# Block 1's lag product moved from the scan stage's lead-in into attention's last unit, and block 1's basis loaded after attention's last transposes

## Chip, cores and metric

The kernel runs on one core of one Trainium2 chip. The metric is device time in microseconds of one execution, taken as the median over several runs of the same built program. The core has five engines with their own instruction streams: PE (matmul), ACT (activations and copies), DVE (vector), POOL (general) and SP, which here only issues DMAs. Engines wait for each other by semaphores. A DMA is issued by the stream of one engine, in the order of that stream; a DMA whose wait isn't met holds up everything behind it on that engine. In this kernel SP and POOL issue nearly all DMAs; what SP issues runs as queue q1, what POOL issues as queue q0.

## What is computed

The reference is forward and backward of a gated sum of two branches over one sequence of 2048 tokens with 576 channels. Its core:

```python
x = A_x
g = _sigmoid((x * gate_w).sum(-1, keepdims=True))
a = _A_ref(x, A_wqkv, A_wo)      # attention, 32 heads of 18
b = _B_ref(x, B_A_re, ..., B_Dskip)   # S4: convolution with a kernel K(d, l)
return g * a + (1 - g) * b
```

`_B_ref` makes for each channel d the kernel `K = einsum("dn,dnl,dn->dl", C, exp(dt*A*l), dt*B).real` with 128 complex states and convolves it with the sequence. The outputs are the value and the gradients of twelve inputs (x, the attention weights, the S4 parameters, the gate), all in bf16.

## The kernel before

The kernel has four stages: projections (to about 150 us of the profiled span), attention forward and backward (to about 2097 us), the S4 branch forward and backward as a chunked scan (to about 2530 us), and a final stage that makes weight gradients and outputs.

**Attention** works in 32 units (8 groups of 4 heads, 4 query blocks of 512 each) of 32 steps. One loop over the step number `G` writes out the instructions of all engines by hand. A unit's backward part runs 39 steps (`OFF`) behind its forward part, so the last unit's backward part fills the steps `NTOT+7` to `NTOT+38`, where `NTOT` is the first step after all forward work. In every step of the backward part PE makes score products (`ps_P`), ACT exponentiates them (`eb`, L1387), and DVE multiplies (`ds`, L1392) the score gradients. The gradient tile of key block `i` (0 to 15, finished every second step) is turned by a DMA transpose on SP (`dsT<-ds`, L1400), 16 of 128x128 for some blocks and 12 for others, where PE turns the rest (`turn_p`, L1095). Its turned form is read by the key-gradient matmuls (`accK`). Finished gradients are turned the same way (`gT`, L1069) and packed and stored by POOL.

**Jobs hung on steps.** Work of the next stage is hung on steps of attention's last unit by `at(("pre", NTOT + x), f)`: f is written out just ahead of step `NTOT + x`, on each engine behind what the earlier steps put there. Memory for it becomes free as pools of attention's tiles are closed (`pt_close`).

**The scan stage** works in 18 blocks of 32 channels. For each block `b` there are:
- `m_load(b)` (L614, L615): the input block `xs` in two DMAs of 512 KB and the gradient block `gyp` of 128 KB. `xs` has one buffer, `gyp` two (by `b % 2`).
- `m_part(b)`: the lag product of the two, 32 matmuls into one bank (`psM`), copied by ACT into `mst` (L628) and written to DRAM as `Md_d` (L629, 288 KB).
- `m_skw(b)` (L641): `Md_d` read back skewed, in four DMAs of 64 KB, into `skw`, which has one buffer.
- `m_sum(b)`: eight small matmuls of `skw`; `m_fin(b)` (L652 to L654): ACT puts their result into the columns of `RX`. `uv(b, h)` (PE, ACT L708) multiplies the turned basis with `RX`, so it follows `m_fin(b)`.
- `load_en(b, h)` (L689): the basis `E1n` of half a block (h = 0, 1), 1 MB; in the lead-in it is issued in four pieces of 256 KB. `turn_e(b, h)` (L671, L672) turns it on PE and copies it out on DVE or ACT. `k0(b)` reads it as well.
- `scan` (DVE L733 to L738): the recurrences, started by `scan_open` (L714). Then `rw1`, `rw2` (DVE L753 `wab`, L758 `Rw`), `pairs1`, `pairs2` (DVE `pq`).
- `t0_load(b)` (L863): the kernel matrix `T0w`, 1 MB, read from `Kp_d`, which `k0_out` has just written.

A **lead-in** ahead of the block loop (L1455 to L1482) brings blocks 0 and 1 up to the scan: `k0(0)`, then the turns, lag sums and `uv` of blocks 0 and 1. There SP's order is written by hand too: the DMAs stand as the lines stand. In the block loop (from L1483) turn `i` scans the second half of block `i` and the first half of block `i + 1`, makes `m_sum(i + 2)`, `m_part(i + 3)`, and loads from POOL.

Before, only block 0's lag product is in attention's last unit: `m_load(0)` at x = 15, `m_part(0)` at 21, `m_skw(0)` at 25. The sixteen pieces of basis of blocks 0 and 1 go out one a step at x = 23 to 38, between the transposes, and `m_load(1)` at x = 40. `m_part(1)` and `m_skw(1)` stand in the lead-in between `turn_e(0, 1)` and `uv(0, 1)`; `m_part(2)` and `m_skw(2)` between `uv(1, 0)` and `uv(1, 1)`.

Of the kernel before, what the change touches and what calls it, by code (L numbers as in the profile page):

```python
# [20 lines left out]
def build(tc, aps, dbg_aps=None, stages=("s1", "attn", "post", "s4", "final")):  # L21
    nc = tc.nc
# [6 lines left out]
    def mm(out, lhsT, rhs, start=True, stop=True, **kw):  # L29
        return nc.tensor.matmul(out, lhsT=lhsT, rhs=rhs, start=start, stop=stop, **kw)  # L30
# [31 lines left out]
    with ExitStack() as gctx:  # L62
# [525 lines left out]
        def load_rx(xb, dma=nc.gpsimd.dma_start):  # L588
            d0 = xb * XB
            RXn = Q["pl"].tile([P, 2 * NB, XB], BF, tag="RXn", bufs=1, name="RXn")  # L590
            dma(RXn[:, 0:NB, :], xr_d[:, :, d0:d0 + XB])
            dma(RXn[:, NB:2 * NB, :], gyr_d[:, :, d0:d0 + XB])
            RXs[xb] = [RXn, None]
# [14 lines left out]
        def m_load(b, dma=nc.gpsimd.dma_start):  # L608
            xs = xss[b] = Q["pl"].tile([P, NSUB, SUB, CB], BF, tag="xs", bufs=1, name="xs")
            n = NSUB // 2  # L610
            for y in range(2):
                src = bass.AP(tensor=xb_d.tensor, offset=xb_d[b:b + 1, y * n:y * n + 1, 0:1].offset,
                              ap=[[XR * SUB * CB, NB], [SUB * CB, NSUB], [1, n * SUB * CB]])
                dma(xs[:, y * n:(y + 1) * n].rearrange("p e t c -> p (e t c)"), src)  # L614
            dma(Q["gyp2"][b % 2][:, SUB:2 * SUB, :].rearrange("p t c -> p (t c)"), gyb_d[b])  # L615

        def m_part(b):
            gyp = Q["gyp2"][b % 2]
            xs = xss[b]
            psM = Q["psM"]()  # L620
            for q in range(4):
                for g_ in range(4):
                    for u in range(2):
                        dd = 8 * q + 2 * g_ + u
                        mm(psM[32 * g_:32 * (g_ + 1), q, :].rearrange("p (e t) -> p e t", t=SUB), lhsT=gyp[:, (1 - u) * SUB:(3 - u) * SUB, dd],
                           rhs=xs[:, ::-1, ::-1, dd], start=(u == 0), stop=(u == 1), tile_position=(0, 32 * g_))
            mst = Q["mst"]
            nc.scalar.copy(mst[:, :, 0:P], psM)  # L628
            Q["mdma"](Md_d[b], mst)  # L629

        def dkp(b):
            return Q["misc2"][b % 2][:, 12 * CB:13 * CB]
# [3 lines left out]
        def m_skw(b):  # L636
            skw = skws[b] = Q["pl"].tile([P, 4, P], F32, tag="skw", name="skw")
            for q in range(4):
                src = bass.AP(tensor=Md_d.tensor, offset=Md_d[b:b + 1, 0:1, q:q + 1, SUB - 1:SUB].offset,
                              ap=[[SUB * 4 * MW, NSUB], [4 * MW - 1, SUB], [1, P]])  # L640
                Q["mdma"](skw[:, q, :], src)  # L641

        def m_sum(b):
            skw = skws.pop(b)
            for v in range(CB // 8):
                mm(dkp(b)[:, v * 8:v * 8 + 8], lhsT=skw[:, v, :], rhs=Q["sel"])

        def m_fin(b):
            RX = RXs[b // 2][1]
            o = (b % 2) * CB  # L650
            pk = dkp(b)
            nc.scalar.copy(RX[:, o:o + CB, CDK], pk)  # L652
            nc.scalar.mul(RX[:, o:o + CB, CDK + 1], pk, Q["l0col"])
            nc.scalar.copy(Q["dDs_row"][:, b * CB:(b + 1) * CB], pk[0:1, :])  # L654

        def blk(b):
            if b not in BK:
                B_ = BK[b] = dict(E={}, En={})
            return BK[b]
# [16 lines left out]
        def load_par(b, dma=nc.gpsimd.dma_start):  # L676
            par = pars_[b] = Q["pl"].tile([P, 10, XB], F32, tag="par", bufs=2, name="par")
            dma(par, par_d[:, 0:10, b * XB:(b + 1) * XB])
# [4 lines left out]
        def load_en(b, h, dma=nc.gpsimd.dma_start, pieces=1):  # L683
            dG = b * CB + h * GS
            En = blk(b)["En"][h] = Q["en", (2 * b + h) % 6 // 2].tile([P, GS, 2, P], BF, tag="E1n", bufs=2, name="E1n")
            n = GS // pieces

            def piece(x):
                dma(En[:, x * n:(x + 1) * n].rearrange("p (g c) r n -> p g (c r n)", c=EQ),  # L689
                    E_d[:, (dG + x * n) // EQ:(dG + (x + 1) * n) // EQ, 0:EQ * 2 * P])  # L690
            piece(0)
            return piece

        def uv(b, h):
            B_ = blk(b)
            if h == 0:
                B_["UV"] = Q["pw"].tile([P, 2, NCOL, CB], BF, tag="UV", bufs=3, name="UV")
            UV = B_["UV"]
            E_ = B_["E"].pop(h)
            RX = RXs[b // 2][1]  # L700
            off = (b % 2) * CB + h * GS
            for q in range(2):
                for ri in range(2):
                    pr = Q["ps"].tile([P, NCOL, 8], F32, tag="bk", bufs=4, name="uvp")
                    for c_ in range(8):
                        mm(pr[:, :, c_], lhsT=E_[:, q * 8 + c_, ri, :], rhs=RX[:, off + q * 8 + c_, :])
                    c0 = h * GS + q * 8
                    nc.scalar.mul(UV[:, ri, :, c0:c0 + 8], pr, -1.0 if ri == 0 else 1.0)  # L708
# [172 lines left out]
        def open_en(x):  # L881
            cm = tc.tile_pool(name=f"s4en{x}", reuse_waits="tile", bufs=1, side="right")
            Q["en", x] = cm.__enter__()
            rights.append(cm)
# [65 lines left out]
        if "attn" in stages:  # L950
# [5 lines left out]
            with ExitStack() as ctx:  # L956
# [157 lines left out]
                NST = 2 * NT  # L1114
                NU = NG * NQ
                OFF = NST + 7
# [4 lines left out]
                def at(n, f):  # L1121
                    todo.setdefault(n, []).append(f)
# [116 lines left out]
                NTOT = NU * NST  # L1239
# [23 lines left out]
                def pt_close(nm, then):  # L1263
                    pts[nm][0].__exit__(None, None, None)
                    then()

                Q["psM"] = lambda: apsp.tile([P, 4, P], F32, tag="accO", name="psM")
                enp = {}

                def en_first(b, h):  # L1270
                    enp[b, h] = load_en(b, h, nc.sync.dma_start, pieces=4)

                for x, f in ((15, lambda: pt_close("a", open_loads)), (15, lambda: m_load(0, nc.sync.dma_start)), (17, lambda: load_rx(0, nc.sync.dma_start)),
                             (21, lambda: m_part(0)), (23, lambda: pt_close("b", lambda: open_en(0))),
                             (25, lambda: m_skw(0)), (31, lambda: pt_close("c", lambda: open_en(1))),
                             (29, lambda: load_par(0, nc.sync.dma_start)), (33, lambda: load_par(1, nc.sync.dma_start)),
                             (OFF + NST // 16 - 1, lambda: m_load(1, nc.sync.dma_start))):
                    at(("pre", NTOT + x), f)
                for q, (b, h) in enumerate(((0, 0), (0, 1), (1, 0), (1, 1))):
                    at(("pre", NTOT + 23 + 4 * q), lambda b=b, h=h: en_first(b, h))  # L1280
                    for y in range(1, 4):
                        at(("pre", NTOT + 23 + 4 * q + y), lambda b=b, h=h, y=y: enp[b, h](y))
                for G in range(NTOT + OFF + 24):
                    now[0] = G
                    for f in todo.pop(("pre", G), []):
# [2 lines left out]
                    if G < NTOT:  # L1288
                        u, s = divmod(G, NST)
                        g, b = units[u]  # L1290
# [11 lines left out]
                    if r1:  # L1302
                        g, b, i, j0 = r1
# [14 lines left out]
                    elif 0 <= m_ < NTOT // 8:  # L1318
                        u_, kq = divmod(m_, NQ)
                        g, b = units[u_]  # L1320
                        if slot in SLOTS:
                            nm, burst, h = SLOTS[slot]
# [17 lines left out]
                    if r2:  # L1340
                        g, b, s2 = r2
# [16 lines left out]
                    if G % 8 in (0, 3, 4, 7) and G >= 3:  # L1358
                        i_ = (G - 3) // 8 * 4 + {3: 0, 4: 1, 7: 2, 0: 3}[G % 8]
                        u_, i_ = divmod(i_, NT)  # L1360
                        if 0 <= u_ < NU:
                            g, b = units[u_]
# [50 lines left out]
        if "s4" in stages:  # L1413
# [8 lines left out]
            with ExitStack() as ctx:  # L1422
# [27 lines left out]
                with tc.manual_schedule(engines={mybir.EngineType.SP}):  # L1450
# [6 lines left out]
                    turn_e(0, 0, 0, 4, dve_copy)  # L1457
                    m_sum(0)
                    m_fin(0)
                    uv(0, 0)  # L1460
                    prep_rx(1, dve_copy)
                    load_rx(1, nc.sync.dma_start)
                    turn_e(0, 1, 0, 4, dve_copy)
                    m_part(1)
                    m_skw(1)
                    m_load(2, nc.sync.dma_start)
                    uv(0, 1)
                    turn_e(1, 0, 0, 4, dve_copy)
                    scan_open(0)
# [1 line left out]
                    turn_e(1, 1, 0, 4)  # L1471
                    m_sum(1)
                    m_fin(1)
                    load_en(2, 1, nc.sync.dma_start)
                    uv(1, 0)
                    m_part(2)
                    m_skw(2)
                    uv(1, 1)
                    scan_open(1)
                    m_load(3, nc.sync.dma_start)  # L1480
                    prep_rx(2)
                    wk_cast(1)  # L1482
                    for i in range(NBLK):  # L1483
# [37 lines left out]
                        if i + 2 >= NBLK:  # L1521
                            y = 2 * (i + 2 - NBLK)
# [348 lines left out]
```

## Time and profile before

| | us |
|---|---|
| median of 3 runs | 2687.24 (2683.43 to 2697.16) |
| the profiled execution | 2685.73 |
| its span, first to last instruction | 2683.9 |

Busy time by stretch, in us, with the granted clock of PE (1.00 is full speed), the busy share of the DMA engines and what they moved:

| stretch | us | PE | DVE | ACT | clock | DMA share | GB/s |
|---|---|---|---|---|---|---|---|
| 150 to 2000, attention | 1850 | 1665.99 | 1647.65 | 1837.72 | 0.99 | 0.85 | 162 |
| 2050 to 2097, its tail | 47 | 28.18 | 26.89 | 18.77 | 0.67 | 1.14 | 237 |
| 2097 to 2146, lead-in | 49 | 32.31 | 27.91 | 24.20 | 0.71 | 0.70 | 177 |
| 2146 to 2530, block loop | 384 | 367.88 | 369.20 | 328.74 | 0.98 | 0.86 | 254 |
| 2530 to 2684, final stage | 154 | 143.76 | 97.96 | 27.07 | 0.98 | 0.87 | 204 |

A share over 1 comes about because packets in flight on one DMA engine overlap. In the rows of the profile, `L1392 DVE ... ds<-ps_P,PT` reads: line 1392 of the kernel, engine, output and inputs, partitions times elements. A bracket `[3.34 <-DMA skw<-Md_d]` behind a row of a timeline is the engine's idle time ahead of it and what ended it. Rows named SPq are SP's issues, with the time from the start of an issue to the next: that includes waiting.

SP's issues around the end of attention, whole lines of its timeline (start, us, what):

```profile
2052.67 1.42 SPq L1400 DMA_TRANSPOSE dsT<-ds  x1
2054.13 1.07 SPq L689 DMA_DIRECT2D E1n<-E_d  x2
2055.30 2.22 SPq L1400 DMA_TRANSPOSE dsT<-ds  x1
2057.61 2.58 SPq L641 DMA_DIRECT2D skw<-Md_d  x4
2065.86 3.99 SPq L1400 DMA_TRANSPOSE dsT<-ds  x1
2090.95 1.82 SPq L1400 DMA_TRANSPOSE dsT<-ds  x1
2092.83 1.96 SPq L614 DMA_DIRECT2D xs<-xb_d  x2
2099.55 0.53 SPq L689 DMA_DIRECT2D E1n<-E_d  x1
2106.87 0.32 SPq L863 DMA_DIRECT2D T0w<-Kp_d  x1
2120.71 2.54 SPq L641 DMA_DIRECT2D skw<-Md_d  x4
```

The transposes, the basis pieces and the loads of the scan stage share this one queue. The row of 2092.83 is `m_load(1)`, the one of 2120.71 is `m_skw(1)`.

### The profile page before, as it was taken

The numbers are of one execution on the slowest core, as the hardware profiler recorded it, in microseconds if no ns is written. First come the engines' busy times: TensorE is split into PE (matmuls) and PEld (weight loads), VectorE is DVE, ScalarE is ACT, GpSimd is POOL, SyncE is SP. The second block draws the span as 40 slices with busy tenths as digits, with TensorE's granted clock in tenths as the row PEclk, the third lists the DMA queues.
The fourth block names the chain that finished last, engine by engine and source line by source line (L and its number), as shares of the span: only waits on it lengthen the run. The fifth ranks groups of instructions, "written<-read, shape, count | busy, mean of one in ns | idle before, by whom it ended". The sixth has DMA issues, their size and how long they took to land.

```text
span 2683.9 us, 69949 instructions
## 1 busy us (share of the span) xinstructions
PE 2404.7 (90%) x27411; PEld 1137.9 (42%) x27411; DVE 2293.8 (85%) x4090; ACT 2350.8 (88%) x2744; POOL 1818.0 (68%) x2829
## 2 busy tenths in 40 slices
PE   8799998998899899889888989989887699999999
PEld 4433333333333333333333333333232499998756
DVE  5648999999989999989999989989897589999964
ACT  5489999999999999999999999999995399999221
POOL 0278888888888888888888888887831045555431
PEclk9879999999999999999999999999996699999999
DMA  7637789879979978997898899789679889998895
GB/s 232 196 99 156 154 159 181 167 153 181 172 152 170 183 160 159 178 172 153 165 178 154 161 172 170 153 163 177 143 140 183 191 244 256 259 262 253 261 261 128
DMA packets 1157013, 486.63 MB, mean 181 GB/s; under 512 B 1071061, under 2 KB 1110598, under 8 KB 1154378
## 3 DMA queue, kind: packets, MB, share of 16 engines
q1 hardware_dynamic: 1110650, 341.49, 64.4%
q0 software_dynamic: 44016, 135.16, 18.3%
q10 hardware_dynamic: 2016, 5.51, 0.6%
q8 instruction: 214, 3.51, 0.6%
q14 instruction: 117, 0.96, 0.1%
HBM read 146.27 MB, written 93.80 MB: 89 GB/s over the span
## 4 chain that ended last, share of the span: by engine, by line
ACT 40%; PE 28%; DVE 18%; issue 6%; DMA 4%; POOL 2%; SPq 1%; ACTq 0%; DVEq 0%; POOLq 0%
ACT eb L1387 23%; ACT PT L1382 14%; DVE ds L1392 7%; PE ps_P L30 7%; PE accV L30 2%; PE ps_dx L30 2%; PE turn_p L1095 2%; PE ps_dwq L30 2%; DVE tz L733 2%; PE ps_proj L30 2%; DVE wab L753 2%; PE yp L30 2%; PE accK L30 1%; DVE dvacc L1149 1%; DVE tz L736 1%
## 5 line engine op out<-in xcount | busy, mean ns | idle before, releaser
L1392 DVE TENSOR_TENSOR ds<-ps_P,PT 128x512 bf16<-128x512 f32 x2048 | 1312.3, 683 | 125.5 <-PE ps_P L30 86.8
L1387 ACT ACTIVATE eb<-ps_P 128x1024 bf16<-128x1024 f32 x1024 | 1099.9, 1074 | 34.8 <-PE ps_P L30 34.5
L1382 ACT ACTIVATE PT<-ps_P 128x1024 bf16<-128x1024 f32 x1024 | 1105.0, 1080 | 21.7 <-PE ps_P L30 20.3
L30 PE MATMUL ps_P<-dOaT,VaT_g 32*128 32x512 bf16 x2048 | 581.9, 388 | 31.5 <-DVE ds L1392 16.1
L506 POOL TENSOR_TENSOR et<-eG,eT 128x448 f32<-128x448 f32 x576 | 542.2, 961 | 10.7
L30 PE MATMUL ps_P<-QaT_g,KaT_g 32*128 32x512 bf16 x2048 | 402.9, 386 | 136.5 <-ACT PT L1382 121.8
L30 PE MATMUL ps_P<-KaT_g,QaT_g 32*128 32x512 bf16 x2048 | 406.0, 389 | 1.6 <-ACT eb L1387 0.6
L30 PEld LDWEIGHTS <-KaT_g 32*128 32x128 bf16 x2048 | 147.6, 91 | 467.5 <-issue 451.4
L506 POOL TENSOR_TENSOR Eo<-et,et 128x448 bf16<-128x448 f32 x288 | 327.0, 1135 | 20.8
L30 PEld LDWEIGHTS <-QaT_g 32*128 32x128 bf16 x2048 | 116.1, 91 | 285.3 <-issue 262.4
L30 PE MATMUL accV<-eb,dOa 128*32 128x512 bf16 x2048 | 185.0, 394 | 27.2 <-ACT eb L1387 27.1
L30 PE MATMUL accO<-PT,Vtok_g 128*32 128x512 bf16 x2048 | 207.4, 394 | 0.0
L30 PE MATMUL accK<-dsT,Qtok_g 128*32 128x256 bf16 x4096 | 162.3, 279 | 14.5 <-DMA dsT<-ds 12.4
L30 PE MATMUL accQ<-ds,Ktok_g 128*32 128x512 bf16 x2048 | 161.6, 394 | 2.3 <-DVE dvacc L1149 2.2
L30 PEld LDWEIGHTS <-Vtok_g 128*32 128x32 bf16 x2048 | 52.7, 93 | 222.7 <-issue 222.7
L1100 DVE COPY dsT<-turn_p 128x1024 bf16<-128x1024 bf16 (+1 forms) x216 | 139.2, 644 | 2.1 <-PE turn_p L1095 2.1
L1095 PE MATMUL turn_p<-ident_bf,ds 128*128 128x128 bf16 x1664 | 134.1, 223 | 1.5 <-DVE gb L1167 0.8
L672 ACT COPY E1e<-etp 128x1024 bf16<-128x1024 bf16 x132 | 125.2, 1059 | 2.6 <-PE etp L671 2.6
L506 POOL TENSOR_TENSOR et<-eT 128x32 f32<-128x32 f32 (+3 forms) x288 | 115.9, 422 | 11.4
L1047 POOL TENSOR_TENSOR dOa<-dO_b,rl 128x288 bf16<-128x288 bf16 x32 | 21.5, 673 | 149.9 <-DVE rl L1042 149.9
L30 PEld LDWEIGHTS <-Qtok_g 128*32 128x32 bf16 x4096 | 87.9, 97 | 79.0 <-issue 64.0
L1095 PEld LDWEIGHTS <-ds 128*128 128x128 bf16 x1664 | 97.3, 99 | 49.5 <-issue 49.5
(294 smaller groups left out, 3749.3 us busy)
## 6 DMA issues: line engine op xcount, KB each, us to landing
E_d<-Eo POOLq DMA_DIRECT2D x144, 256.0 KB, 3.4
E1n<-E_d POOLq DMA_DIRECT2D x30, 1024.0 KB, 7.3
T0w<-Kp_d SPq DMA_DIRECT2D x18, 1024.0 KB
xs<-xb_d POOLq DMA_DIRECT2D x28, 512.0 KB, 9.8
dsT<-ds SPq DMA_TRANSPOSE x512
dqkv_d<-dtk POOLq DMA_DIRECT2D x96, 72.0 KB, 4.2
Md_d<-mst SPq DMA_DIRECT2D x18, 288.0 KB
skw<-Md_d SPq DMA_DIRECT2D x72, 64.0 KB
```

What stands on the lines that cost most here:

```text
L30: return nc.tensor.matmul(out, lhsT=lhsT, rhs=rhs, start=start, stop=stop, **kw)
L506: nc.gpsimd.tensor_tensor(out, a, b, op=op)
L672: copy(E_[:, 4 * q:4 * q + 4], pt_)
L733: nc.vector.tensor_tensor(tz[x], HG[:, :, k - 1].unsqueeze(1).to_broadcast([P, 2, 2, n, CB]), ZZ.unsqueeze(3).to_broadcast([P, 2, 2, n, CB ...
L736: nc.vector.tensor_tensor(tz[x][:, 0], tz[x][:, 0], UVk[:, :, :, k, :], op=A.add)
L753: nc.vector.tensor_tensor(wab, h_, w_, op=A.mult)
L1095: nc.tensor.transpose(pt_[:, x, qb, :], t_[:, qb * P:(qb + 1) * P], ident_bf)
L1100: (nc.scalar.copy if NTOT <= now[0] < NTOT + OFF else nc.vector.tensor_copy)(o_(), pt_[:, x:x + n])
L1149: nc.vector.tensor_tensor(o_, a_, acc, op=A.add)
L1382: nc.scalar.activation(U["PT"][i, j // 2], ps, ACT.Exp)
L1387: nc.scalar.activation(e, ps, ACT.Exp)
L1392: nc.vector.tensor_tensor(U["ds"][i][:, j, :], ps, U["PT"][i, j // 2][:, j % 2, :], op=A.mult)
```

## The change

Three things move; no instruction is added on PE, ACT, DVE or POOL, and SP issues the same DMAs in another order.

1. `m_load(1)` goes from x = 40 to x = 23, `m_part(1)` from the lead-in to x = 31, `m_load(2)` from the lead-in to x = 33.
2. The basis pieces of block 0 move one step later (x = 24 to 31), those of block 1 from x = 31 to 38 to x = 41 to 48, which is behind the last transpose of score gradients (step 38).
3. In the lead-in `m_skw(1)` stands behind `m_fin(0)`, `m_part(2)` and `m_load(3)` stand where `m_part(1)` and `m_load(2)` stood, `m_skw(2)` behind `m_fin(1)`; between `uv(1, 0)` and `uv(1, 1)` no lag product is left.

On SP the order from step 23 on becomes: `xs`, `xs`, `gyp` of block 1, the pieces of block 0 between the transposes, `Md_d` of block 1 between the transposes of i = 11 and i = 12, `xs`, `xs`, `gyp` of block 2 ahead of that of i = 13, then the last transposes, then block 1's eight pieces with three `gT` transposes between them, `E1n` of block 2, `Kp_d`, `T0w`, `skw` of block 1, `RXn`, `Md_d` of block 2, the load of block 3, `skw` of block 2.

```diff
                              (29, lambda: load_par(0, nc.sync.dma_start)), (33, lambda: load_par(1, nc.sync.dma_start)),
-                             (OFF + NST // 16 - 1, lambda: m_load(1, nc.sync.dma_start))):
+                             (23, lambda: m_load(1, nc.sync.dma_start)),
+                             (31, lambda: m_part(1)), (33, lambda: m_load(2, nc.sync.dma_start))):
                     at(("pre", NTOT + x), f)
                 for q, (b, h) in enumerate(((0, 0), (0, 1), (1, 0), (1, 1))):
-                    at(("pre", NTOT + 23 + 4 * q), lambda b=b, h=h: en_first(b, h))
+                    at(("pre", NTOT + 24 + 4 * q + 9 * (q // 2)), lambda b=b, h=h: en_first(b, h))
                     for y in range(1, 4):
-                        at(("pre", NTOT + 23 + 4 * q + y), lambda b=b, h=h, y=y: enp[b, h](y))
+                        at(("pre", NTOT + 24 + 4 * q + 9 * (q // 2) + y), lambda b=b, h=h, y=y: enp[b, h](y))
...
                     m_fin(0)
+                    m_skw(1)
                     uv(0, 0)
                     prep_rx(1, dve_copy)
                     load_rx(1, nc.sync.dma_start)
                     turn_e(0, 1, 0, 4, dve_copy)
-                    m_part(1)
-                    m_skw(1)
-                    m_load(2, nc.sync.dma_start)
+                    m_part(2)
+                    m_load(3, nc.sync.dma_start)
                     uv(0, 1)
...
                     m_fin(1)
+                    m_skw(2)
                     load_en(2, 1, nc.sync.dma_start)
                     uv(1, 0)
-                    m_part(2)
-                    m_skw(2)
                     uv(1, 1)
                     scan_open(1)
-                    m_load(3, nc.sync.dma_start)
                     prep_rx(2)
```

## The prediction

> **What bounds the kernel now.** The change touches only the handover from attention to the scan stage, about 2050 to 2146 us of the span, so I read three views of that stretch: the chain of waits, the timelines of PE and DVE, and the windows of ten microseconds. I call the moment when attention's last key-gradient matmul starts E0 (2096.24 us here).
>
> ```profile
> 2073.01 4.45 DMA dsT<-ds
> 2077.50 1.07 PE accK L30 x15
> 2089.66 1.20 SPq L1069
> 2090.95 5.24 DMA dsT<-ds
> 2115.67 4.96 DMA Md_d<-mst
> 2120.71 2.50 DMA skw<-Md_d
> 2139.39 6.51 DMA gyp<-gyb_d
> ```
>
> Here (start, us, what) the attention tail waits twice for a turned score gradient on SP's queue, and the lead-in waits on block 1's lag chain (write Md_d, read it back skewed as skw) and on the load of block 3's basis.
>
> ```profile
> 2077.50 1.04 PE L30 MATMUL accK<-dsT,Qtok_g 128*32 128x256 bf16 x16 [6.27 <-DMA dsT<-ds]
> 2096.24 1.04 PE L30 MATMUL accK<-dsT,Qtok_g 128*32 128x256 bf16 x16 [4.92 <-DMA dsT<-ds]
> 2123.24 0.39 PE L30 MATMUL misc<-sel,skw 128*128 128x8 f32 x2 [3.34 <-DMA skw<-Md_d]
> 2126.57 3.57 PE L30 MATMUL uvp<-RX,E1e 128*128 128x64 bf16 x32 [0.58 <-ACT dDs_row L654]
> 2145.94 2.13 PE L30 MATMUL psM<-xs,gyp 128*32 128x128 bf16 x32 [5.20 <-DMA gyp<-gyb_d]
> 2135.75 0.42 DVE L733 TENSOR_TENSOR tz<-HG,par 128x256 f32<-128x256 f32 x1 [9.17 <-ACT HG L714]
> 2162.83 0.42 DVE L733 TENSOR_TENSOR tz<-HG,par 128x256 f32<-128x256 f32 x1 [3.81 <-ACT HG L714]
> ```
>
> The brackets are idle time of the engine before the row and what ended it. DVE's two waits are the result: the block loop starts when DVE starts block 1's scan (2135.75), and its first turn is long. The wab rows start at 2145.78, 2172.86, 2194.78 and 2216.30 in the DVE timeline and the chain: 27.1 us for turn 0, then 21.9 and 21.5.
>
> ```profile
> 2060.00:2070.00 10.00, 7.72 (x65) 1.68 (x66) 8.76 (x15) 6.91 (x7) 1.18 (x2) 0.80 1.00 206
> 2070.00:2080.00 10.00, 3.49 (x47) 1.52 (x36) 3.21 (x6) 1.90 (x2) 1.18 (x2) 0.50 1.16 266
> 2080.00:2090.00 10.00, 7.27 (x49) 2.10 (x47) 4.94 (x8) 2.60 (x4) 1.18 (x2) 0.50 1.24 261
> 2110.00:2120.00 10.00, 9.90 (x166) 8.76 (x164) 5.69 (x13) 7.26 (x11) 1.18 (x2) 0.98 0.56 128
> 2120.00:2130.00 10.00, 5.54 (x40) 5.13 (x40) 6.55 (x41) 4.59 (x9) 0.00 (x0) 0.70 0.64 156
> ```
>
> The last three columns are clock, DMA share and GB/s. In the tail the DMA engines are full (share 1.00 to 1.24) and PE is not (3.49 of 10 us); in the lead-in it is the other way round. So whatever bytes the change puts into the tail are paid there, and whatever waits it takes out of the lead-in are gained.
>
> **The change part by part.** All terms are against the profiled run, 2685.73 us (span 2683.9 and 1.8 around it).
>
> *Tail, up to the first stall (T11, the landing at 2077.46).* Ahead of it SP now issues block 1's load (two xs of 512 KB and gyp of 128 KB) and one basis piece of 256 KB fewer: 896 KB or 0.92 MB more. At 206 to 266 GB/s that is 3.5 to 4.5 us. On SP itself the rows of the same load at 2035.42 and 2137.60 (1.95 for two xs, 0.41 for gyp) less one piece (0.5) give 1.9 us. SP has about 0.8 us to give: the transpose at 2055.30 took 2.22 us against 1.42 for the one before it, waiting for DVE. So T11 comes 1 to 4.5 us later. I take 3.5, nearer the DMA end, because the share is full there.
>
> *m_part(1) in the tail.* 32 matmuls, 2.1 us on PE by the row of m_part(0) (2044.24, 2.13), and 0.59 on ACT, both at step 31, before the stall of 6.27 us, which hides them. If that stall were gone they would cost 1.7: the score steps around m_part(0) stood 3.69 apart (2043.17 to 2046.86) where the same pair a block of eight steps later took 1.99. Their write Md_d is new on SP ahead of the 13th transpose of the unit (row i = 12) and waits for ACT's mst. Behind it stand one basis piece, that transpose, par and block 2's load. PE reaches step 31 near 2062 and SP reaches the write near 2079, so I cost the wait at nothing; if xs(1) landed late, SP, PE and the last four transposes would wait for it, one for one.
>
> *Tail, T11 to E0.* Added: block 2's load and Md_d, 1152 + 288 KB. Gone: seven basis pieces, 1792 KB. That is 352 KB (0.36 MB) less, 1.4 us at 263 GB/s. SP issues three or four short DMAs (2.4 + 0.5 us) in place of seven (0.5 each), 0.6 us less. But block 2's load goes in one lump before the last three transposes, so I take only 0.5 off. The floor is PE's own work: from T11 to where PE stood ready for its last matmul was 13.9 us (2096.24 − 4.92 − 2077.46) where the row took 18.8; 4.9 us is the most that can be won. E0 shift: +3.5 − 0.5 = **+3.0** (ends +4.5, and 1 − 4.9 = −3.9).
>
> The Trainium skill, "DMA: Bandwidth & Descriptors", section "Anatomy of one DMA", gives a DMA's variable part as bytes over 436 GB/s, and its section on queues and rings says each engine consumes descriptors in ring order. The order speaks against this change, since the loads stand in front of the transposes. By that bandwidth the first term would be 2.1 in place of 3.5 and the sum 1.4 us lower; the rows never show more than 266 GB/s here, so I stay with the rows.
>
> *Block 1's basis behind the last transpose.* 2 MB, first used by the turns at 2116.09, 19.9 us after E0. Six pieces go out right behind the last transpose, two behind the dkacc transpose (2098.27 to 2099.46). At 221 to 248 GB/s 2.1 MB take 8.5 to 9.5 us from 2092.8, so they land near 2103, some 10 us before use. Cost 0; beyond that cover each us late costs one.
>
> *Block 1's chain out of the lead-in.* m_part(2) takes m_part(1)'s place at 2112.30 at the same 2.1 us. skw(1) is now issued right behind the load of T0w, which waits for Kp_d (landed 2106.8 before; I assume 2 us more). Its four issues (2.5) and landing (2 more, behind T0w's 1 MB) end near E0 + 18; m_sum(1) wants them at 2119.91 (E0 + 23.7). So the waits of 3.34, 0.48 and 0.15 go. Next late is ACT: its turn copies end at 2122.31, m_fin adds 0.6, so uv(1,0) starts near 2122.9 instead of 2126.57: **3.6** gained. Queued behind skw(1) on SP are RXn, Md_d(2) and block 3's load, all of which waited for ACT until 2113.5 or later anyway.
>
> *m_part(2) and clock out of the last pair.* Before, from uv(1,0) at 2126.57 to HG at 2135.42 were 8.85 us, holding one uv at the half clock (3.57; the other 1.96) and psM (0.47 + 2.11). Without them two uv and ACT's copies take about 4.8 (from uv at 2114.32 the first four copies ended 2.7 us later, another four take 2.1). At the slow clock it is 6.4. Gain 2.4 to 4.0, I take **3.7**, since the stall that lowered the clock is gone.
>
> *Turn 0 of the loop.* Block 3's load is issued after m_part(2) (near 2115 to 2119 instead of 2138.16) and skw(2) after m_sum(1), so m_sum(2) (3.44 + 0.27) and psM (5.20) no longer wait; hR and gR then reach DVE in time (its pq rows waited 1.3 and 0.8) and so does block 2's HG (3.81). Turn 0 falls from 27.1 to the 21.5 of the later turns: **5.6**; if ACT's 4 us of RX copies hold it, 3. POOL issues the same things in the same order and only earlier.
>
> Sum: 3.6 + 3.7 + 5.6 = 12.9 gained after E0, 3.0 lost before it, 9.9 net: 2685.73 − 9.9 = 2675.8. The loop's turns are DVE-bound at 21.5 us afterwards, so nothing takes the gain back. The median of the runs (2683.43, 2687.24, 2697.16) lies 1.5 above the profiled run; I forecast **2677**. Own range: gain 9 to 13 less −3.9 to 4.5, so 2670 to 2682 on the median's side.
>
> **The rivals.** *The tail gets shorter.* For it: SP issues without a break from 2057, and seven issues leave the second part. Against: the DMA share. Then T11 comes 1.5 later and the second part loses 4.5: −3.0 and −12.9 from 2687.2 give 2671.
>
> *skw(1) is late behind T0w.* SP is in order, T0w already waited 4.8 us for Kp_d, and Kp_d now follows 3 MB of basis. Landed at E0 + 18 instead of + 12.6, skw(1) costs its 3.6, and Md_d(2), xs(3) and skw(2) slide with it, another 2 of turn 0: 2687.2 − 9.9 + 5.6 = 2683. Against: the margin of 5.7 us.
>
> *The loads hold the transposes for their whole landing (the slower side).* Place: the two xs/gyp loads in SP's ring ahead of row 8 and rows 13 to 15. In the lead-in such a load took 7.2 us from issue (2123.35) to use (2130.61), Md_d 4.96. Two loads and the write in series are 19.4; eight pieces less at 1.0 (256 KB at 263 GB/s) leave 11.4, and m_part(1) uncovered adds 1.7: E0 + 13.1, which takes back all 12.9. It is slower once a load holds the ring over 7.1 us; at 8 us it reads 2689. Against: landing includes latency that overlaps.
>
> *It does not do what it says.* The order on the engines shows PE, ACT and SP moved as told, so this is left out.
>
> **How the numbers follow.** Forecast 0.54, shorter tail 0.24, late skw 0.14, slower side 0.08. A measurement of this kernel tells about 0.5%, 13.4 us, from no change: faster is below 2673.8, slower above 2700.7. Faster: most of the shorter tail (0.18) and a sixth of the forecast (0.09), 0.27. Slower by that much: 0.03, the far end of the last case. Same 0.70. The range takes 2668 (both ends of gain) to 2686, leaving the slower side and some of the shorter tail out.
>
> **What would show it.** T11's stall grows from 6.27 to some 10 us, less the 2.1 of psM, and E0 stands near 2099. No skw wait before m_sum(1), no gyp wait before the third and fourth psM; wab(0) near E0 + 42.3 (was 49.5) and wab(1) 21.5 later. I am wrong if E0 lies below 2096 or above 2101, if turn 0 stays above 24 us, or if PE waits for block 1's basis near E0 + 20.

## The result and the profile after

| | before | after |
|---|---|---|
| median of 18 runs each, us | 2690.8 (2680.12 to 2697.16) | 2679.89 (2672.95 to 2692.3) |
| ratio, with its 95% interval | | 0.9968 (0.9955 to 0.998) |
| the profiled execution, us | 2685.73 | 2685.84 |

The interval is 5.4 to 12.1 us below the time before: a gain, and within half a per cent. The two profiled executions agree to 0.1 us by chance. In that of after, the projections end 6.5 us later (first `PT` on ACT at 138.11 against 131.56) and attention's body, up to block 0's lag product, takes 4.5 us longer (1917.2 against 1912.7). The change touches neither, and over the fourteen profiled executions of this study the two scatter by 9 and 17 us. So I compare stages, from marks in the timelines: `psM0` is the start of block 0's lag product on PE, T11 and E0 are those of the prediction, wab(0) and wab(1) the starts of DVE's first two `wab`. Where the last two groups of accK stand in one row of 32 matmuls, E0 is the start of the second. Here `after` is the profiled execution of the result and two more (r1, r2 below).

| us | psM0 to T11 | T11 to E0 | lead-in, E0 to wab(0) | turn 0, to wab(1) | psM0 to wab(1) |
|---|---|---|---|---|---|
| before | 33.3 | 18.7 | 49.5 | 27.1 | 128.6 |
| after | 36.5 | 19.2 | 40.6 | 22.4 | 118.7 |
| after, r1 | 37.9 | 19.4 | 43.1 | 22.4 | 122.8 |
| after, r2 | 35.9 | 18.0 | 44.2 | 21.2 | 119.3 |
| mean of after less before | +3.5 | +0.1 | -6.9 | -5.1 | -8.4 |

The time from wab(1) to wab(17) is 343.2 before and 342.7 to 343.6 after, so nothing is given back in the loop.

The three executions of the same kernel differ by 3.6 us in the lead-in. Four groups of matmuls at its start show why: the turns of the basis (`etp`), m_sum(0), uv(0, 0) and the next `etp` are the same work each time, but PE's clock comes back at a different one of them.

| us | etp | m_sum(0) | uv(0, 0) | etp | E0 to uv(1, 0) | lead-in |
|---|---|---|---|---|---|---|
| before | 3.57 | 1.82 | 3.55 | 2.01 | 30.3 | 49.5 |
| after | 3.23 | 1.01 | 1.95 | 1.98 | 24.1 | 40.6 |
| after, r1 | 3.57 | 1.82 | 3.33 | 1.98 | 26.7 | 43.1 |
| after, r2 | 3.57 | 1.82 | 3.57 | 3.25 | 28.0 | 44.2 |

The granted clock of the first 12 us from E0 is 0.67 in after, 0.50 in r1 and in r2; before it is 0.50 (2096 to 2107). The four groups add up to 2.5 us more in r1 than in after and 4.0 more in r2, and uv(1, 0) starts 2.5 and 3.9 us later. Only r1 has nearly the clock of before: against it the change gains 3.7 us up to uv(1, 0) and 6.4 in the lead-in. Of the 9.0 that the profiled execution of after shows, some 2.5 are the clock's and not the change's.

PE's timeline of after (start, us, what, and in brackets the idle time ahead and what ended it):

```profile
2091.82 1.04 PE L30 MATMUL accK<-dsT,Qtok_g 128*32 128x256 bf16 x16 [7.64 <-DMA dsT<-ds]
...
2105.32 1.04 PE L30 MATMUL accK<-dsT,Qtok_g 128*32 128x256 bf16 x16 [1.57 <-DMA dsT<-ds]
...
2110.99 1.04 PE L30 MATMUL accK<-dsT,Qtok_g 128*32 128x256 bf16 x16 [4.62 <-DMA dsT<-ds]
...
2132.12 1.01 PE L30 MATMUL misc<-sel,skw 128*128 128x8 f32 x8
...
2135.12 5.36 PE L30 MATMUL uvp<-RX,E1e 128*128 128x64 bf16 x64 [2.00 <-ACT dDs_row L654]
...
2141.20 0.39 PE L30 MATMUL misc<-sel,skw 128*128 128x8 f32 x2 [0.72 <-DMA skw<-Md_d]
...
2143.48 2.17 PE L30 MATMUL psM<-xs,gyp 128*32 128x128 bf16 x32
```

The stalls of the tail are still there (6.27 has become 7.64, 4.92 has become 1.57 and 4.62). What is gone is in the lead-in: m_sum(1) at 2132.12 has no bracket where it had 3.34, m_sum(2) waits 0.72 instead of 3.44, and block 3's lag product at 2143.48 has no bracket where it had 5.20. What uv(1, 0) now waits for is ACT, as forecast. Of the chain of waits, the pieces for Md_d, skw and gyp are no longer among the longest. In the tail one piece for `dsT` is left (4.54 us); behind it the chain now runs over a transpose `gT<-dkacc` (5.15) and two stores `dqkv_d<-dtk` (4.75 and 4.35) to uv(0, 0). PE's bracket at uv(0, 0) is 0.58 for ACT before and after, so these stores are not seen to cost anything.

DVE's timeline of after, the two waits that answer to 9.17 and 3.81 before, and SP's in the same execution:

```profile
2141.52 0.43 DVE L733 TENSOR_TENSOR tz<-HG,par 128x256 f32<-128x256 f32 x1 [2.56 <-ACT HG L714]
2163.96 0.43 DVE L733 TENSOR_TENSOR tz<-HG,par 128x256 f32<-128x256 f32 x1 [1.25 <-ACT HG L714]
```

```profile
2098.55 6.21 SPq L1401 DMA_TRANSPOSE dsT<-ds  x2
...
2124.88 0.32 SPq L863 DMA_DIRECT2D T0w<-Kp_d  x1
2125.30 2.52 SPq L641 DMA_DIRECT2D skw<-Md_d  x4
```

The row of 2098.55 is where block 2's load is paid for in the tail: the two transposes right behind block 2's load took 6.21 us to issue. `T0w` goes out at E0 + 13.9: SP waited 6.9 us there for Kp_d (4.8 before), which now has 2 MB more of basis ahead of it. skw(1) goes out right behind it and is there when m_sum(1) wants it at E0 + 21. With the 2 us of landing that the prediction took, the margin is an estimated 2.3 us where 5.7 was forecast: it is the thin place of the kernel, as two experiments show.

### The profile page after: what moved, and what is told of

Same layout as the page of the kernel before. It is cut to its first block, busy times and chain, and to the rows that moved or that the text cites. A ratio compares the mean times of both kernels' runs of the same rounds, so it can differ in the third digit from the quotient of the medians.

```text
span 2684.0 us, 69947 instructions
## 1 busy us (share of the span) xinstructions
PE 2401.6 (89%) x27411; PEld 1138.0 (42%) x27411; DVE 2293.6 (85%) x4090; ACT 2351.5 (88%) x2744; POOL 1821.7 (68%) x2829
## 3 DMA queue, kind: packets, MB, share of 16 engines
q0 software_dynamic: 44016, 135.16, 18.7%
## 4 chain that ended last, share of the span: by engine, by line
ACT 40%; PE 26%; DVE 21%; issue 6%; DMA 3%; POOL 2%; SPq 1%; ACTq 0%; DVEq 0%; POOLq 0%
ACT eb L1388 23%; ACT PT L1383 14%; DVE ds L1393 7%; PE ps_P L30 7%; DVE tz L733 3%; DVE wab L753 3%; PE accV L30 2%; PE turn_p L1095 2%; PE ps_dx L30 2%; PE ps_proj L30 2%; DVE tz L736 2%; DVE HG L738 2%; PE yp L30 1%; DVE Rw L758 1%; DVE dvacc L1149 1%
## 5 line engine op out<-in xcount | busy, mean ns | idle before, releaser
L30 PE MATMUL accV<-eb,dOa 128*32 128x512 bf16 x2048 | 183.9, 392 | 27.4 <-ACT eb L1388 27.1
```

## The experiments

All edits are against the changed kernel unless another is named. Medians of runs are beside those of the kernel before on the same chip; a single run is named as such.

**The changed kernel again**, twice.

> The changed kernel once more, unaltered, for how far a stage repeats. I cut the span at four marks: the start of the first psM (the last unit, 2044.24 us before, 2055.29 after), E0 (start of the last accK), and the wab rows of turns 0 and 1. Before: tail 52.0, lead-in 49.5, turn 0 27.1. After: 55.7, 40.6, 22.4. If the change's effect sits in these three stages and the rest is scatter between executions, all three repeat within 1 us (55.7, 40.6, 22.4), while the time to the first psM does not stay at 2055 but falls anywhere from 2040 to 2057. If the change itself lengthened the stages ahead of it, the first psM stands near 2055 again.

> The changed kernel once more, beside the variants on one chip, for their comparison: 0.996 to 0.998 of the kernel before; first part of the tail 36 to 38 us, second 19, lead-in 40.5 to 43, turn 0 22.4.

r1: 2686.24 us, one run (before 2693.3). r2: 2683.89 (before 2691.73), ratio 0.9969 (0.9949 to 0.999). The stages are in the table above; in r1 and r2 the lead-in is 43.1 and 44.2, not 40.6, so a stage does not repeat within the 1 us expected. The first lag product stands at 2050.75 and 2054.55, within the scatter of the stages ahead.

**Block 2's load behind the last turned score gradient**, run twice.

```diff
-                             (31, lambda: m_part(1)), (33, lambda: m_load(2, nc.sync.dma_start))):
+                             (31, lambda: m_part(1)), (40, lambda: m_load(2, nc.sync.dma_start))):
```

> Only block 2's load (xs, xs, gyp, 1152 KB) goes from step 33 to step 40, behind the last transposes and ahead of block 1's basis. Theory (bytes and issues ahead of the last transposes on SP's queue set the tail): from the landing after the first stall to E0 falls from 19.2 to 14 or 15 (PE's own work is 13.9), the tail from 55.7 to about 51, lead-in stays 40.6 or grows by up to 2 as the basis lands later, turn 0 22.4; time 3 to 5 us below the changed kernel. Rival (the transposes' own latency and SP's issue times set it, the load is hidden): the tail stays 55 to 56 and the time the same.

> The changed kernel with block 2's load behind the last turned score gradient, once more, for its size: theory (its 1.15 MB ahead of the last transposes cost 4 us of tail): 4 to 5 us below the changed kernel, second part of the tail 15 us. Rival (the first measurement was favoured by its executions): within 2 us of the changed kernel in the median, with the second part of the tail at 15 us all the same and the gain lost elsewhere.

2675.57 us (before 2693.3), ratio 0.9941 (0.9918 to 0.9964); then 2679.3 (before 2691.73), ratio 0.9956 (0.9937 to 0.9974). PE's timeline of the first:

```profile
2092.79 1.04 PE L30 MATMUL accK<-dsT,Qtok_g 128*32 128x256 bf16 x16 [0.85 <-DVE dsT L1100]
2095.01 1.04 PE L30 MATMUL accK<-dsT,Qtok_g 128*32 128x256 bf16 x16 [1.17 <-DMA dsT<-ds]
...
2128.66 2.36 PE L30 MATMUL misc<-sel,skw 128*128 128x8 f32 x8 [2.42 <-DMA skw<-Md_d]
```

T11 to E0 falls to 15.0 us, and to 13.9 in the second execution, which is PE's own work (13.9 by the prediction's floor). So block 2's load, 1152 KB ahead of the last three transposes, cost the change 4 to 5 us. On SP the two transposes that took 6.21 us to issue in after take half of it (3.25 in the second execution):

```profile
2085.26 3.00 SPq L1401 DMA_TRANSPOSE dsT<-ds  x2
```

The profile puts 4.2 us of the 6.21 down to DVE's `gb`; here the same issues ended at 2088.26, ahead of `gb` (2090.18), so it was not `gb` that held them. The second execution gives some of the gain back in the lead-in (44.9 us, in the first 42.6): T0w goes out at E0 + 19.0, PE's clock is back early (uv(0, 0) at 1.95), and m_sum(1) waited 2.41 for skw. In the first PE is slower (uv(0, 0) at 3.57), m_sum(1) finds skw there, and the 2.42 in the row of 2128.66 is m_sum(2)'s. In both, uv(1, 0) starts at E0 + 27.5. The second expectation's "4 to 5 below" held on that chip: 2683.89 less 2679.3 is 4.6, though the two intervals overlap.

**The basis of block 1 ahead of the last transposes again.**

```diff
-                    at(("pre", NTOT + 24 + 4 * q + 9 * (q // 2)), lambda b=b, h=h: en_first(b, h))
+                    at(("pre", NTOT + 24 + 4 * q), lambda b=b, h=h: en_first(b, h))
...
-                        at(("pre", NTOT + 24 + 4 * q + 9 * (q // 2) + y), lambda b=b, h=h, y=y: enp[b, h](y))
+                        at(("pre", NTOT + 24 + 4 * q + y), lambda b=b, h=h, y=y: enp[b, h](y))
```

> The changed kernel with block 1's eight basis pieces at steps 32 to 39 again, so ahead of or between the last transposes; the loads stay. Theory (bytes set the tail): 1792 KB more ahead of the last transpose, at 263 GB/s 6.8 us, so the second part of the tail grows from 19.2 to 24 to 27 and the tail to 60 to 63; lead-in 40 to 41; time 5 to 8 us over the changed kernel, about where the kernel before is. Rival (basis pieces fit into gaps): tail 55 to 57.

2676.34 us, one run (before 2693.3). T11 to E0 becomes 23.5 us (two stalls for `dsT<-ds`, 4.74 and this one of 5.75), the lead-in 39.5, from psM0 to wab(1) 121.2 us, no other than after's 118.7 to 122.8.

```profile
2102.83 1.04 PE L30 MATMUL accK<-dsT,Qtok_g 128*32 128x256 bf16 x16 [5.75 <-DMA dsT<-ds]
```

Behind T11 the basis costs about 4.5 us, where 6.8 was expected from its bytes; the 5 to 8 us over the changed kernel did not come. The lead-in is 3 us below the mean of after, but the queue is not shown to give that back: T0w goes out at E0 + 10.4 instead of 13.9, yet uv(1, 0) still waits 2.00 for ACT and starts at E0 + 24.5, close to the profiled after (24.1). What is shorter is the pair of uv behind it, 3.73 us against 5.36 on PE, at a granted clock of 1.00 against 0.72.

**Before, with the move of block 1's basis alone.**

```diff
-                    at(("pre", NTOT + 23 + 4 * q), lambda b=b, h=h: en_first(b, h))
+                    at(("pre", NTOT + 23 + 4 * q + 10 * (q // 2)), lambda b=b, h=h: en_first(b, h))
...
-                        at(("pre", NTOT + 23 + 4 * q + y), lambda b=b, h=h, y=y: enp[b, h](y))
+                        at(("pre", NTOT + 23 + 4 * q + 10 * (q // 2) + y), lambda b=b, h=h, y=y: enp[b, h](y))
```

> The kernel before with block 1's basis alone moved behind the last transposes and behind block 1's load; the lag chain stays in the lead-in. Theory: first part of the tail unchanged (33.3), second part falls from 18.7 to 14 or 15, so the tail is 47.5 to 49; lead-in stays 49.5 (its waits for skw and gyp are there) or 1 to 2 more since SP has eight more issues in it; turn 0 27; time 2 to 4 us below the kernel before. If the whole gain of the change came from the basis move, it would be 8 us below.

2689.62 us (before 2693.3), ratio 0.9996 (0.998 to 1.0013): nothing. PE's timeline, then SP's:

```profile
2108.14 1.90 PE L30 MATMUL accK<-dsT,Qtok_g 128*32 128x256 bf16 x32 [0.85 <-DVE l0col L1431]
...
2138.07 0.60 PE L30 MATMUL misc<-sel,skw 128*128 128x8 f32 x2 [6.76 <-DMA skw<-Md_d]
```

```profile
2125.54 0.32 SPq L863 DMA_DIRECT2D T0w<-Kp_d  x1
...
2135.48 2.54 SPq L641 DMA_DIRECT2D skw<-Md_d  x4
```

The last two accK groups run together without a wait (T11 to E0 13.7 us, 5 less). But Kp_d stands behind the basis, T0w goes out 8.3 us after Kp_d's issue (5.2 before), skw(1) at 2135.48, and m_sum(1) waits 6.76 instead of 3.34: the lead-in is 52.5 us, 3 more. A transfer taken out of one queue position was paid for at the next. With the run before this says that the gain of the change is that of the lag chain and not of the basis.

**The loads of blocks 1 and 2 issued by POOL.**

```diff
-                             (23, lambda: m_load(1, nc.sync.dma_start)),
-                             (31, lambda: m_part(1)), (33, lambda: m_load(2, nc.sync.dma_start))):
+                             (23, lambda: m_load(1)),
+                             (31, lambda: m_part(1)), (33, lambda: m_load(2))):
```

> The changed kernel with the loads of blocks 1 and 2 (xs, xs, gyp each) issued by POOL at the same steps instead of by SP, so that the same bytes move at the same time but the score-gradient transposes no longer stand behind them in SP's queue. Theory A (what counts in the tail is the bytes in flight): the stretch from block 0's lag product to E0 stays at 56 to 57 us (first part, to the 11th transpose, 36 to 38; second part some 19) and the time stays within 1 us of the changed kernel. Theory B (the order in SP's queue is what the transposes pay): the second part falls to 15 and the first to 34 to 36, so the tail to 50 to 52 us, and the time falls by 4 to 6 us to about 2674 (before at 2689).

2684.88 us (before 2695.89), ratio 0.997 (0.9948 to 0.9991), no other than after. The tail is 57.9 us (after 53.9 to 57.3), but cut otherwise: 43.1 to T11 and 14.8 behind it. One premise was wrong: POOL issued the loads earlier than SP does, block 1's 7.0 us after psM0 and block 2's 27.1 us after it (on SP 10.6 and 39.8). So the last transposes were free and the earlier ones paid (stalls of 5.55 and 8.79 up to T11). Which transposes wait depends on what moves ahead of them; the length of the tail stays as it was. The windows from psM0 to E0 go with that (width, busy time and number by engine, then clock, DMA share, GB/s), in the order before, after, block 2's load behind, loads on POOL:

```profile
2044.00:2096.00 52.00, 32.26 (x320) 11.29 (x320) 29.94 (x48) 22.74 (x24) 6.52 (x12) 0.70 1.18 233
```

```profile
2055.00:2111.00 56.00, 35.03 (x355) 13.25 (x355) 29.74 (x48) 23.24 (x25) 6.49 (x12) 0.65 1.15 230
```

```profile
2044.00:2095.00 51.00, 36.29 (x352) 13.10 (x351) 30.13 (x48) 23.56 (x25) 7.06 (x12) 0.63 1.16 232
```

```profile
2046.00:2104.00 58.00, 34.66 (x356) 12.77 (x356) 29.84 (x48) 23.29 (x25) 10.45 (x18) 0.68 1.17 225
```

The rate is 225 to 233 GB/s in all four while the length differs: 52 us times 233 GB/s is 12.1 MB, then 12.9, 11.8 and 13.1 MB. That speaks for the bytes, but does not prove them, since each product is made with the length itself, and the kernel with the basis ahead moved 242 GB/s over 60 us (14.5 MB).

**Block 3's load back behind the opening of block 1's scan.**

```diff
                     m_part(2)
-                    m_load(3, nc.sync.dma_start)
                     uv(0, 1)
...
                     scan_open(1)
+                    m_load(3, nc.sync.dma_start)
                     prep_rx(2)
```

> The changed kernel with block 3's load put back behind the opening of block 1's scan, where it stood before. Theory (the early load of block 3 is what shortened turn 0): the lag product of block 3 waits some 5 us for gyp again, turn 0 goes from 22.4 to 25 to 27 us, the lead-in stays at 40.5 to 43, the time is 3 to 5 us above the changed kernel. Rival (turn 0 was shortened by the earlier skw of block 2 and by the higher clock alone): turn 0 stays at 22 to 23 us, the wait for gyp is hidden behind DVE's recurrences.

2688.19 us, one run (before 2695.89). The wait is back:

```profile
2150.42 2.13 PE L30 MATMUL psM<-xs,gyp 128*32 128x128 bf16 x32 [7.63 <-DMA gyp<-gyb_d]
```

Yet turn 0 is only 24.2 us against a mean of 22.0 (21.2 to 22.4): 2.2 of the 7.6 us reach DVE. So the early load is worth about 2 of the 5.1 us that turn 0 lost, below the 2.6 to 4.6 expected; that the other 3 come from skw(2) and from block 2's lag product being out of the pair is left over by subtraction, not shown.

**The skewed read of block 1 back behind the lag product that now stands there.**

```diff
                     m_fin(0)
-                    m_skw(1)
                     uv(0, 0)
...
                     m_part(2)
+                    m_skw(1)
                     m_load(3, nc.sync.dma_start)
```

> The changed kernel with the skewed read of block 1 issued behind the lag product of block 2 in the lead-in, where it stood before, and not ahead of it. Theory (the place of this read in SP's order is what the lead-in gained by): the read stands behind RXn and Md_d of block 2, m_sum(1) waits 3 to 6 us for skw, the lead-in goes from 40.6 to 43 up to 44 to 47 us. Rival (ACT's copies of the turned basis set when uv(1, 0) starts, not skw): the wait appears but the lead-in grows by no more than 1 us.

2689.27 us, one run (before 2695.89). The wait returns, 3.60 and then 1.53:

```profile
2134.38 1.46 PE L30 MATMUL misc<-sel,skw 128*128 128x8 f32 x6 [3.60 <-DMA skw<-Md_d]
```

The lead-in is 45.3 us, 2.7 above the mean of after and 1.1 above the longest of them. But PE's first four groups took 3.29, 1.01, 1.95 and 1.98, the clock of the profiled after, and against that execution the lead-in is 4.8 longer and uv(1, 0) 4.9 later (E0 + 29.0). That is the theory's size. PE's bracket of 2.00 for ACT falls to 0.58 in exchange, so a part of the wait was ACT's anyway. It is one run.

**Block 2's load behind, and wk's cast ahead of RX on ACT.** The edit comes on top of block 2's load behind. PE waits 2 to 2.5 us for `wk` right behind E0, before and after.

```diff
+                    wk_cast(0)
                     prep_rx(0, dve_copy)
                     load_en(2, 0, nc.sync.dma_start)
-                    wk_cast(0)
```

> The changed kernel with block 2's load behind the last turned score gradient (as in the experiment that put it there) and, in the lead-in, ACT's cast of wk for block 0 ahead of the preparation of RX of block 0, so that the kernel matrix of block 0 need not wait 2.0 to 2.5 us for it. Theory (PE's wait for wk stands on the path from E0 to the scan): the lead-in is 2 us shorter than the 42.6 us with block 2's load behind alone, about 40.5; tail 50 to 51; time some 2 us below that run, about 17 to 19 below the kernel before. Rival (the wait goes to the next thing ACT makes late, RX or its turn copies): the lead-in stays at 42 to 43 and the time is that of block 2's load behind alone, 15 to 16 below before.

2684.19 us (before 2695.89), ratio 0.995 (0.9933 to 0.9968): the rival. The wait for wk is gone, and PE comes earlier to the next one:

```profile
2135.49 1.20 PE L30 MATMUL misc<-sel,skw 128*128 128x8 f32 x6 [2.53 <-DMA skw<-Md_d]
```

The lead-in is 43.8 us. skw(1) stands behind the issue of T0w, which waited for Kp_d until 2130.04, E0 + 18.2:

```profile
2130.04 0.32 SPq L863 DMA_DIRECT2D T0w<-Kp_d  x1
```

**T0w behind block 3's load**, on top of that.

```diff
                     k0_out(0)
-                    t0_load(0)
                     turn_e(0, 0, 0, 4, dve_copy)
...
                     m_load(3, nc.sync.dma_start)
+                    t0_load(0)
                     uv(0, 1)
```

> The kernel with block 2's load behind the last turned score gradient and wk's cast first, and with the load of block 0's kernel matrix T0w moved on SP behind block 3's load, so that the skewed read of block 1 no longer stands behind the wait for Kp_d. Theory (with wk first, SP's wait for Kp_d is what m_sum(1) pays): m_sum(1) no longer waits for skw (2.5 + 0.5 us in the run with wk first), the next to set uv(1, 0) are ACT's turn copies, the lead-in falls by 2 us from 43.8 to about 41.8, m_sum(2) does not wait, the time falls by some 2 us against the run with wk first. Rival (the lead-in at the half clock is PE's own work and ACT's): the wait goes but the lead-in and the time stay within 1 us. T0w lands some 8 us later than before and is read only 27 us after its issue, so its move itself costs nothing.

2675.99 us (before 2691.73), ratio 0.9949 (0.9932 to 0.9967). m_sum(1) does not wait beyond 0.17, and the lead-in is 38.0 us: 5.8 less than the last, where 2 was expected. Part of that is PE's clock: its first two groups behind k0 took 3.25 and 1.01 instead of 3.57 and 1.82, the next uv 1.95 instead of 3.27, 2.5 us in all, so the move itself is worth some 3.3. But 1 MB is now ahead of skw(2), which brought a wait into turn 0 (24.2 us):

```profile
2125.19 2.34 PE L30 MATMUL misc<-sel,skw 128*128 128x8 f32 x8 [5.50 <-DMA skw<-Md_d]
```

**T0w behind skw(2) too.**

```diff
                     m_load(3, nc.sync.dma_start)
-                    t0_load(0)
                     uv(0, 1)
...
                     m_skw(2)
+                    t0_load(0)
```

> The last kernel (block 2's load behind, wk first, T0w behind block 3's load) with T0w moved on SP one step further, behind the skewed read of block 2. Theory (skw of block 2 landed 5.5 us late because 1 MB of T0w was put ahead of it): m_sum(2)'s wait of 5.50 us goes to under 2, turn 0 falls from 24.2 to 21.2, lead-in stays at 38 to 40, tail 49 to 51; from block 0's lag product to the scan's second rw1 109 to 111 us (before 128.6, changed kernel 118.7 to 122.8); time 2 to 3 us below that kernel, some 16 to 19 below the kernel before. T0w is then issued near E0 + 27 and read near E0 + 43. Rival (skw of block 2 is late because of block 3's load ahead of it, 1.15 MB): the wait stays at 4 us or more and turn 0 at 23 to 24.

2676.98 us (before 2692.95), ratio 0.9939 (0.9917 to 0.9961). m_sum(2)'s wait goes to 2.09, turn 0 to 22.4, the lead-in stays at 37.9, and psM0 to wab(1) is 111.0 us, 17.6 less than before and 9.3 less than the mean of after. Part of it is lost at the end: from wab(17) to the end 171.2 us, 172.3 in the run before, where before and the three executions of after have 166.4 to 168.2 (one of the two with block 2's load behind has 169.9, so not all of it is clear of scatter). PE's timeline of the last kernel:

```profile
2552.30 0.66 PE L30 MATMUL ps_a<-wo_sb,OT 128*128 128x288 bf16 x2 [3.80 <-DMA OT<-O_tok]
```

After has no such wait. SP's first load of the final stage (`zA`) went out 4.2 us after wab(17) in this kernel, and 8.2 ahead of it in before and after; `O_tok` went out 5.7 us later than in after, measured from wab(17), and the turned `OT` follows it. SP waited there for DVE's wab. I think that the later place of T0w gave another tile its memory, which zA has to wait for; that was not tried.

By its ratio this is the fastest measured here, about 16 us below before, 8 more than the change. Its interval overlaps those of the variants with block 2's load behind, so which of those is best is not settled, nor are the 2 to 3 us expected against the last kernel; that they lie below the changed kernel rests on ratios of 0.9939 and 0.9968, whose intervals overlap by 0.0006, and on the stages, which agree.

## Why the prediction was right

The forecast was 2677 with a gain of 9.9; measured are 2679.89 and a gain of 10.9 between the medians, 8.6 by the ratio and 8.4 by the stages. The mechanism is the one forecast: the tail pays some 3.6 us, and the lead-in and turn 0 gain 12.0 where 12.9 was expected. The absolute figure owes something to luck: the median of before went from 2687.24 (3 runs) to 2690.8 (18 runs), and the stages gained 1.5 less than forecast. Point by point:

- *T11 later by 3.5 (1 to 4.5).* Mean 3.5 (2.6 to 4.6). The stall of 6.27 "to some 10 less the 2.1 of psM" is 7.64 to 8.68 in the three executions. The Trainium skill, "DMA: Bandwidth & Descriptors", section "Anatomy of one DMA — SWDGE (gpsimd) path", gives bytes over 436 GB/s for a DMA issued on the gpsimd path; an estimate by that figure is 2.1. These loads are issued by SP, and the 3.5 measured is nearer to what the windows' 225 to 233 GB/s give (3.9 to 4.1 for 0.92 MB).
- *T11 to E0, 0.5 less.* Mean 0.1 more (18.0 to 19.4). Two larger terms cancel: of block 2's load I said that it "goes in one lump before the last three transposes" and took only 0.5 for the balance; the lump costs 4 to 5 us, and the basis that left was worth about 4.5. The shorter tail of the rival shows with block 2's load at x = 40 instead of 33.
- *E0 shift +3.0.* Mean +3.6. The absolute mark that I gave (E0 "near 2099", wrong above 2101) failed: it reads 2110.99, since psM0 alone came 11 us later than before. A mark has to be measured from the start of its own stage.
- *m_part(1) hidden in the tail, 0.* Its row (2074.51 in after) stands ahead of the stall of 7.64.
- *Basis behind the last transposes, 0.* PE never waited for block 1's basis. But the basis alone does make Kp_d later (SP waits 6.9 to 7.2 for it instead of 4.8), which costs nothing only because skw(1) left its old place: in the kernel with the basis moved alone it cost 3.
- *skw(1)'s wait out of the lead-in, 3.6.* From E0 to uv(1, 0) was 30.3 and is 24.1, 26.7 and 28.0: 4.1 in the mean, 3.7 against r1, which has nearly the clock of before. ACT sets it, as forecast (bracket 2.00 in all three).
- *psM and the clock out of the last pair, 3.7.* From uv(1, 0) to wab(0) was 19.2 and is 16.2 to 16.4: 2.8 to 3.0. This term was mis-sized, and its reason, that "the stall that lowered the clock is gone", did not hold. I took about 4.8 us from uv(1, 0) to HG, and 6.4 at the slow clock; it took 6.1, 6.1 and 5.8. Both uv together took 5.36, 5.36 and 4.99 us on PE, where two at the full clock are 3.9; PE still stood 2.00 us for ACT just ahead of them, and the granted clock over the pair was 0.72 in after.
- *Turn 0, 5.6.* Mean 5.1. m_sum(2) still waits for skw, 1.2 in all in after, not in r1 and r2.
- *Late skw and the loads that hold the transposes.* Neither showed in the changed kernel: SP's wait for Kp_d ended at E0 + 13.9, not + 18. But the late skw is real a short way off: T0w goes out at E0 + 17 to 19 in the kernels with block 2's load behind, and in two of these three executions m_sum(1) waited for skw.
- *Two readings of rows.* The row of 2139.39 is `gyp`, the gradient block of block 3's load, and not a basis; the row of `gyp` given as 2137.60 is that of 2037.60. No term rests on either slip.

## What to carry to other kernels

Where the DMA engines are full and PE is not, as in this tail, a load moved into the stretch costs time: here 3.5 us for 0.92 MB, 4 to 5 for 1.2 MB, 4.5 for 1.8 MB, so roughly by the measured rate or less. Issuing it from another engine did not save it; other transposes waited. So move what removes a chain of waits elsewhere (here the lag chain), and place bulk loads behind the last transfer that an engine waits for. When an issue that waits (T0w behind Kp_d) stands ahead of a small read on an in-order queue, the read inherits the wait: let the small, early-ready one pass first, and look for the next thing behind it. Before a difference of a few us between two executions is put down to a change, see whether PE's clock came back at the same group in both.

## What was not expected of the hardware

PE's half clock is worth as much as most of the waits treated here. At the start of the lead-in the same 32 turns of the basis (`etp`) took 3.20 to 3.57 us, where at full clock they take 1.98. In the profiled after the clock came back three groups earlier than in r2 (m_sum(0) 1.01 against 1.82, uv(0, 0) 1.95 against 3.57, the next `etp` 1.98 against 3.25), and r2's lead-in is 3.7 us longer. The mean granted clock from psM0 to E0 was 0.63 to 0.70 in the four windows shown.

The share of busy DMA engines read 1.15 to 1.18 in those windows at 225 to 233 GB/s, while the block loop reached 256 GB/s at 0.86 (2151 to 2536 of after): the share says that the engines are taken, not that bytes move at their best.
